# Transposing q and k on VectorE instead of TensorE in a windowed-attention and MLP kernel

## The chip, the cores and the metric

The kernel runs on one core of one Trainium2 chip. The metric is the time of one execution on the device in microseconds (us). The kernel before takes 755.5 us, the median of three runs (754.73 to 755.7).

The engines have the names of the profile: PE is TensorE (PEld its weight loads), DVE is VectorE, ACT is ScalarE, POOL is GpSimd, and SP is the engine whose queue issues nearly all DMAs.

## The reference

q, k and v have the shape (4 batches, 8 heads, 768 positions, 64), all float32. Attention is causal over a window of 128 positions, with the first 4 positions (the "sinks") always visible. The result goes through an MLP with 512 inputs and 2048 hidden units.

```
scores = scale * np.matmul(q, k.transpose(0, 1, 3, 2))
keep = is_sink | ((rel >= 0) & (rel < int(window)))
scores = np.where(keep, scores, -1000000000.0)
a = np.exp(scores - np.max(scores, axis=-1, keepdims=True))
a = a / (np.sum(a, axis=-1, keepdims=True) + 1e-09)
attn_out = np.matmul(a, v)                       # (B, H, S, D)
x = attn_out.transpose(0, 2, 1, 3).reshape(B * S, H * D)
h = x @ w_in
out = (h * (1.0 / (1.0 + np.exp(-h)))) @ w_out
```

## The kernel before

**Tiling.** The 4 x 768 rows of x are cut into eight *chunks* of 384 rows (CT = 384; a chunk is one half of one batch). Attention of a chunk is done in four *pairs* of heads, so there are 32 pairs, p = 0 to 31. The MLP of a chunk runs over 16 blocks of 128 hidden units (fc). For each block, `mlp1` (L834 to L846) makes 12 matmuls of 384 columns into an `h` tile, `act` (L848) lets ACT and DVE apply the activation, and `mlp2` (L860) adds 9 matmuls of 512 columns into three output banks. Each float32 product is split into a high and a low part in a narrower float32 format (fp32r), hence three matmuls where one would be expected.

**Two kinds of pair.** Pairs 0 to 7 (the first two chunks) go through functions whose names begin with `f_`; the change does not touch these functions. Pairs 8 to 31, the last six chunks, go through `load`, `q_prep`, `k_prep`, `v_prep`, `scores`, `softmax`, `ptrans`, `strans` and `av`. While the MLP of chunk c runs, the attention of chunk c + 2 runs between its matmuls.

**q and k.** `load` (L344) brings q and k of the two heads of a pair into SBUF as they lie in memory: a position on each of the 128 partitions, three blocks of positions for q (tile `qn`) and three or four for k (tile `kn`, four where the chunk is the second half of its batch and needs 128 keys of the first), and for each position the 64 numbers of one head beside the 64 of the other. The scores need the head dimension on the partitions. So `q_prep` (L381) has PE transpose each 128 x 128 block into the PSUM tile `qt` (L385), by a matmul against the identity, and `k_prep` (L402) does the same into `kt` (L408). ACT then copies the high parts from PSUM (L394, L395 for q; L422, L423 for k), and DVE subtracts them to get the low parts (L396, L397; L424, L425). For q, two more copies (L399, L400) fill the other half of `qd`. `scores` (L461, L465) are matmuls on these tiles.

**Buffers.** `qn` and `kn` have one buffer each, so a load of the next pair can start only when the transposes of this pair have read them. `qt`, `kt`, the score tiles, the transposed probabilities (`pt`, `sk`) and the attention outputs (`o`) share one PSUM tag, `at`, with three buffers that go round in the order in which the tiles are asked for.

**Order.** Each step is put on a list with a time (`at`), in units of one hidden block of the MLP (sixteen units to a chunk, four to a pair). The list is sorted by time and the steps are recorded in that order; a scheduling layer then fixes each engine's sequence of instructions, and at run time an engine never changes this sequence. The times are those in the table `OPT`: `a` has the offsets of the steps of a pair from that pair's own time T (`q`, `k`, `s` for the scores, `sm` for the softmax, `st` for `strans`, `av0` and `av1` for the two heads' outputs); `tk` the time at which the sinks are fetched; `wc` and `wcd` the start and the step of 32 range checks of the weights (`wchk`), each with a DMA of 512 KB and work on DVE and ACT.

Of the kernel before, what the change touches and what calls it, by code (L numbers as in the profile page):

```python
# [8 lines left out]
F32 = mybir.dt.float32  # L9
# [16 lines left out]

OPT = dict(
    S=7.834, s0=0.903, f_l=2.468, f_p=-1.643, f_v=3.079, f_sm=0.693, f_pt=0.795, f_av=0.052,
    tk=14.143, s1=1.65, F1=1.021, D0=2.076, w=[0.458, 8.623, 11.237, 18.219], wd=[0.839, 0.58,
    1.293, 0.683], wc=15.613, wcd=2.766, warm=7, wg=4, ord=1, edge=8, dua=15, adp=0, glp=0,  # L30
    ptv=9, fill=[0, 4, 0, 0, 1, 1, 0, 2], na=[2, 16], lod=[6, 30], a=dict(load=-2.705, q=0.041,
    k=-0.274, v=1.959, s=1.338, sd=0.33, sm=1.66, smd=0.624, pt0=3.456, st=3.466, pt1=3.482,
    av0=4.25, av1=4.394), m0=dict(act=0.606, m2=2.061), m=dict(act=0.378, m2=1.546), fin=0.692,
)


# [134 lines left out]
def attn_moe_kernel(  # L171
# [11 lines left out]
    nc = tc.nc  # L183
    B, H, S, D = q.shape
# [5 lines left out]
    P = 128  # L190
    HP = H // 2
    CT = 384
    NTB = CT // P
# [10 lines left out]
    ident = const.tile([P, P], F32, name="ident")  # L204
    make_identity(nc, ident)

    warm = OPT["warm"]
# [23 lines left out]
    with ExitStack() as fast:  # L231
        wpool = fast.enter_context(tc.tile_pool(name="wpool", bufs=1))
        p1 = fast.enter_context(tc.tile_pool(name="p1", bufs=1))
# [6 lines left out]
        m0 = p1.tile([P, P], F32, name="m0")  # L240
        m1 = p1.tile([P, WIN], F32, name="m1")
        m2 = p1.tile([P, WIN], F32, name="m2")
# [89 lines left out]
        st = [dict() for _ in range(NPER)]  # L332
# [6 lines left out]
        def geo(p):  # L339
            c, hp = divmod(p, HP)  # L340
            b, half = turns[c]
            return c, b, half, hp

        def load(p):  # L344
            c, b, half, hp = geo(p)
            s = st[p]
            r0 = half * CT
            s["qn"] = p1.tile([P, NTB, 2, D], F32, tag="qn", name=f"qn{p}")
            s["kn"] = p1.tile([P, NTB + 1, 2, D], F32, tag="kn", name=f"kn{p}")
            j0 = 0 if half else 1  # L350
            rk = r0 - P if half else r0
            for j in range(2):
                h = 2 * hp + j
                nc.sync.dma_start(
                    s["qn"][:, :, j, :], q[b, h, r0 : r0 + CT].rearrange("(t p) d -> p t d", p=P)
                )
                nc.sync.dma_start(
                    s["kn"][:, j0:, j, :], k[b, h, rk : r0 + CT].rearrange("(t p) d -> p t d", p=P)
                )

        def load_v(p):
            c, b, half, hp = geo(p)
# [18 lines left out]
        def q_prep(p):  # L381
            s = st[p]
            qt = ps_a.tile([P, 512], F32, tag="at", name=f"qt{p}")
            for t in range(NTB):
                nc.tensor.transpose(  # L385
                    qt[:, t * P : (t + 1) * P], s["qn"][:, t].rearrange("p h d -> p (h d)"), ident
                )
            qd = p1.tile([P, 2, CT], F32R, tag="qd", name=f"qd{p}")
            if "low" not in zero:
                zero["low"] = p1.tile([P, 2, CT], F32R, tag="ql", name="qlz")  # L390
                nc.gpsimd.memset(zero["low"].bitcast(F32), 0.0)
            ql = zero["low"]
            s["qd"] = qd
            nc.scalar.copy(qd[0:64, 0], qt[0:64, :CT])  # L394
            nc.scalar.copy(qd[64:128, 1], qt[64:128, :CT])  # L395
            nc.vector.tensor_tensor(ql[0:64, 0], qt[0:64, :CT], qd[0:64, 0], ALU.subtract)  # L396
            nc.vector.tensor_tensor(ql[64:128, 1], qt[64:128, :CT], qd[64:128, 1], ALU.subtract)  # L397
            eng = nc.gpsimd if p < OPT["dua"] else nc.vector
            eng.tensor_copy(qd[64:128, 0], qd[0:64, 0])  # L399
            eng.tensor_copy(qd[0:64, 1], qd[64:128, 1])  # L400

        def k_prep(p):  # L402
            c, b, half, hp = geo(p)
            s = st[p]
            j0 = 0 if half else 1
            kt = ps_a.tile([P, NTB + 1, P], F32, tag="at", name=f"kt{p}")
            for j in range(j0, NTB + 1):
                nc.tensor.transpose(  # L408
                    kt[:, j], s["kn"][:, j].rearrange("p h d -> p (h d)"), ident
                )  # L410
            ks = p1.tile([P, 2, (NTB + 1) * SEG], F32R, tag="ks", name=f"ks{p}")
            s["ks"] = ks
            ksv = ks.rearrange("p h (j c) -> p h j c", c=SEG)
            for j, src in ((0, ksA), (1, ksB)):
                n = NTB - j0
                nc.gpsimd.tensor_copy(  # L416
                    ksv[:, j, j0:NTB, P:],
                    src[:, hp, b, :].unsqueeze(1).to_broadcast([P, n, NS]),
                )
            A = ksv[:, 0, j0:, :P]  # L420
            Bk = ksv[:, 1, j0:, :P]
            nc.scalar.copy(A[0:64], kt[0:64, j0:])  # L422
            nc.scalar.copy(Bk[64:128], kt[64:128, j0:])  # L423
            nc.vector.tensor_tensor(A[64:128], kt[0:64, j0:], A[0:64], ALU.subtract)  # L424
            nc.vector.tensor_tensor(Bk[0:64], kt[64:128, j0:], Bk[64:128], ALU.subtract)  # L425
# [494 lines left out]
        for p in range(NPER):  # L920
            T = O["S"] + 4.0 * (p - HP)
            c, b, half, hp = geo(p)
# [26 lines left out]
            tl = T - 4.0 + max(A["k"] + 0.05, 4.0 + A["load"])  # L949
            tv = T - 4.0 + max(A["v"] + 0.05, 4.0 + A["load"])  # L950
            at(tl, lambda p=p: load(p))
            at(tv, lambda p=p: load_v(p))
            if hp == 0 and (c == 2 or b != turns[c - 1][0]):
                at(max(tv, O["tk"]) + 0.02, lambda b=b: load_vs(b))
            at(T + A["q"], lambda p=p: q_prep(p))
            at(T + A["k"], lambda p=p: k_prep(p))
            at(T + A["v"], lambda p=p: v_prep(p))
            for j in range(2):
# [12 lines left out]
        D0 = O["D0"]  # L971
# [51 lines left out]
```

## Time and profile before

| | before |
|---|---|
| median of three runs | 755.5 us (754.73 to 755.7) |
| profiled execution | 756.05 us |
| its span, first to last instruction | 754.3 us |
| granted TensorE clock, mean | 0.996 |
| busy: PE, PEld | 736.4 us (98%), 651.0 us (86%) |
| busy: DVE, ACT, POOL | 545.0 us (72%), 522.6 us (69%), 256.8 us (34%) |
| DMA | 98837 packets, 61.87 MB |

The span has three stages. Up to 139 us the eight early pairs are computed, the weights are read and split, and the MLP of the first chunk begins. From 139 us, where the first of the later pairs starts, to 682 us, where the seventh chunk is finished, the MLP and the later pairs run side by side. The last 72 us have the MLP of the last chunk alone.

One caution on PE rows: a matmul's duration in the profile runs from its start to its modelled end, and the next one starts before that end. What a matmul costs a busy PE is the distance from its start to the next start, not its duration.

### The profile page before, as it was taken

How to read it: one execution, taken by the hardware profiler on the slowest of the kernel's cores; microseconds unless marked ns; L12 is line 12 of the kernel's file. 1: busy time of each engine (PE TensorE's matmuls, PEld its weight loads, DVE VectorE, ACT ScalarE, POOL GpSimd, SP SyncE). 2: the span in 40 equal slices, each digit the busy share in tenths (PEclk: the TensorE clock that was granted, in tenths of full speed). 3: DMA queues.
4: the chain of work that ended last, by engine and by line, in shares of the span. 5: the costliest groups of instructions: out<-in, count | busy, mean ns of one | idle time of the engine just before them, and what ended most of it. 6: DMA issues, size and time to landing. Idle time of an engine off the chain costs nothing.

```text
span 754.3 us, 12661 instructions
## 1 busy us (share of the span) xinstructions
PE 736.4 (98%) x4068; PEld 651.0 (86%) x4068; DVE 545.0 (72%) x1435; ACT 522.6 (69%) x1195; POOL 256.8 (34%) x549
## 2 busy tenths in 40 slices
PE   7998999999999999999999999999999999999996
PEld 5676778789999999998999988999899999999885
DVE  5889788979767886678876797777876787752222
ACT  4879888588776776777866787767776777642222
POOL 3310000345454564534434453443433434330000
PEclk9999999999999999999999999999999999999999
DMA  7556454544111521025211450115311211001001
GB/s 177 167 153 182 129 152 146 159 132 149 27 41 40 168 78 36 20 69 159 70 40 40 123 150 16 34 32 153 112 35 39 84 39 40 1 1 43 0 1 44
DMA packets 98837, 61.87 MB, mean 82 GB/s; under 512 B 87504, under 2 KB 87504, under 8 KB 98768
## 3 DMA queue, kind: packets, MB, share of 16 engines
q1 hardware_dynamic: 98480, 61.03, 28.8%
q8 instruction: 33, 0.54, 0.3%
q14 instruction: 36, 0.29, 0.1%
q10 hardware_dynamic: 288, 0.00, 0.0%
HBM read 54.72 MB, written 6.29 MB: 81 GB/s over the span
## 4 chain that ended last, share of the span: by engine, by line
PE 81%; DVE 8%; DMA 4%; ACT 3%; issue 2%; SPq 1%; POOL 0%; DVEq 0%
PE h L843 30%; PE out L870 11%; PE out L871 11%; PE out L869 10%; PE o L574 3%; PE o L780 3%; DMA wraw<-in_moe_w_in_dram 2%; PE s L461 2%; PE s L465 2%; PE pt L516 2%; DMA wchk<-in_moe_w_out_dram 2%; PE s L715 1%; PE kt L408 1%; PE sk L547 1%; PE o L590 1%
## 5 line engine op out<-in xcount | busy, mean ns | idle before, releaser
L843 PE MATMUL h<-xh,winh 128*128 128x384 f32 x512 | 176.4, 345 | 0.0
L843 PE MATMUL h<-xl,winh 128*128 128x384 f32 x512 | 173.7, 339 | 0.0
L843 PE MATMUL h<-xh,winl 128*128 128x384 f32 x512 | 173.6, 339 | 0.0
L869 PE MATMUL out<-wouth,gh 128*128 128x512 f32 x384 | 152.9, 401 | 2.4 <-ACT gh L855 2.3
L870 PE MATMUL out<-wouth,gl 128*128 128x512 f32 x384 | 153.4, 400 | 0.6 <-DVE gl L857 0.6
L871 PE MATMUL out<-woutl,gh 128*128 128x512 f32 x384 | 153.0, 398 | 0.0
L854 DVE TENSOR_TENSOR sg<-h,sg 128x384 f32<-128x384 f32 x128 | 70.8, 554 | 82.4 <-ACT sg L853 81.4
L853 ACT ACTIVATE sg<-h 128x384 f32<-128x384 f32 x128 | 62.9, 492 | 81.4 <-PE h L843 79.4
L857 DVE TENSOR_TENSOR gl<-sg,gh 128x384 fp32r<-128x384 f32 x128 | 79.0, 617 | 31.2 <-ACT gh L855 29.5
L843 PEld LDWEIGHTS h<-xh,winh 128*128 128x128 f32 x512 | 96.5, 189 | 4.4 <-issue 0.6
L843 PEld LDWEIGHTS h<-xl,winh 128*128 128x128 f32 x512 | 96.3, 188 | 3.2
L843 PEld LDWEIGHTS h<-xh,winl 128*128 128x128 f32 x512 | 96.0, 188 | 1.1 <-issue 0.9
L855 ACT CAST gh<-sg 128x384 fp32r<-128x384 f32 x128 | 65.3, 510 | 39.1 <-DVE sg L854 37.7
L871 PEld LDWEIGHTS out<-woutl,gh 128*128 128x128 f32 x384 | 72.6, 189 | 17.2 <-issue 0.5
L869 PEld LDWEIGHTS out<-wouth,gh 128*128 128x128 f32 x384 | 72.0, 188 | 14.8 <-ACT gh L855 3.0
L870 PEld LDWEIGHTS out<-wouth,gl 128*128 128x128 f32 x384 | 72.7, 189 | 14.0 <-DVE gl L857 1.8
L532 POOL TENSOR_SCALAR_AFFINE_SELECT pq<-pq 128x384 fp32r<-128x384 f32 (+1 forms) x96 | 53.9, 570 | 63.0 <-ACT pq L525 63.0
L482 ACT ACTIVATE pm<-pm,mx 128x264 f32<-128x264 f32 (+1 forms) x144 | 71.3, 496 | 4.9 <-DVE mx L469 3.0
L502 POOL TENSOR_SCALAR pm<-pm,r 128x128 f32<-128x128 f32 x144 | 56.4, 409 | 34.4 <-DVE r L487 21.4
L469 DVE CUSTOM_DVE_ANT_0 pm<-s,m 128x264 f32<-128x264 f32 (+1 forms) x144 | 54.5, 408 | 13.2 <-PE s L465 12.7
L437 POOL TENSOR_TENSOR vs<-vn,vs 128x256 fp32r<-128x256 f32 (+1 forms) x48 | 35.4, 746 | 84.0 <-ACT vs L435 75.7
L416 POOL CAST ks<-ksA 128x24 fp32r<-128x24 f32 (+1 forms) x24 | 9.1, 378 | 160.6 <-PE s L465 98.7
(167 smaller groups left out, 1394.9 us busy)
## 6 DMA issues: line engine op xcount, KB each, us to landing
wraw<-in_moe_w_in_dram SPq DMA_DIRECT2D x16, 512.0 KB
wraw<-in_moe_w_out_dram SPq DMA_DIRECT2D x16, 512.0 KB
wchk<-in_moe_w_in_dram SPq DMA_DIRECT2D x16, 512.0 KB
wchk<-in_moe_w_out_dram SPq DMA_DIRECT2D x16, 512.0 KB
qn<-in_q_dram SPq DMA_DIRECT2D x64, 96.0 KB
kn<-in_k_dram SPq DMA_DIRECT2D x32, 128.0 KB
vn<-in_v_dram SPq DMA_DIRECT2D x32, 128.0 KB
out_dram<-ost SPq DMA_DIRECT2D x7, 512.0 KB
```

What stands on the lines that cost most here:

```text
L469: nc.vector.tensor_tensor_reduce(out=pm[:, t, off:], in0=sp[:, :w], in1=(m0, m1, m2)[min(blk, 2)], scale=-0.125, scalar=3.0e38, op0=ALU.ad ...
L482: nc.scalar.activation(x, x, AF.Exp, bias=mx[:, p, j * NTB + t : j * NTB + t + 1], scale=-1.0, accum_out=r[:, t : t + 1],)
L502: nc.gpsimd.tensor_scalar(x, x, r[:, t : t + 1], 1.0, ALU.mult, ALU.mult)
L532: nc.gpsimd.affine_select(out=before, in_=own, pattern=[[0, n], [-1, P]], compare_op=ALU.is_gt, fill=0.0, base=0, channel_multiplier=1,)
L843: nc.tensor.matmul(hps[:, :CT], w[g][:, cc, fs], s[x], start=n == 0, stop=n == 3 * NCC - 1)
L853: nc.scalar.activation(sg, hps[:, :CT], AF.Sigmoid)
L854: nc.vector.tensor_tensor(sg, hps[:, :CT], sg, ALU.mult)
L855: nc.scalar.copy(gh, sg)
L857: eng.tensor_tensor(gl, sg, gh, ALU.subtract)
L869: nc.tensor.matmul(o, gh[:, ts_], wout_h[g][:, f], start=fc == 0, stop=False)
L870: nc.tensor.matmul(o, gl[:, ts_], wout_h[g][:, f], start=False, stop=False)
L871: nc.tensor.matmul(o, gh[:, ts_], wout_l[g][:, f], start=False, stop=fc == NFC - 1)
```

## The change

`load` now cuts each head's 64 numbers into two halves of 32, and positions into blocks of 32. A DMA takes one half of one head: position within its block goes to 32 partitions, block number and the 32 numbers go along the row. Four DMAs each for q and k (two before) put the four groups of 32 head dimensions under one another. A run that lies together in memory is now 32 numbers long (128 bytes) where it was 64 (256 bytes). VectorE's transpose works on 32 x 32 blocks, each in its place; on this layout it gives what PE's transposes gave, head dimension on the partition and position along the row, in the same PSUM tiles `qt` and `kt`. So `q_prep` has one DVE instruction instead of three PE transposes, `k_prep` one instead of three or four. The rest of both functions is as it was. The table of times has new values: among them q's preparation is placed 0.61 units earlier and k's 0.2 later than before (below); `tk` goes from 14.143 to 16.284 and `wc` from 15.613 to 18.17, and `av0`, `av1` and `fin` by less than 0.5.

```diff
-    ptv=9, fill=[0, 4, 0, 0, 1, 1, 0, 2], na=[2, 16], lod=[6, 30], a=dict(load=-2.705, q=0.041,
-    k=-0.274, v=1.959, s=1.338, sd=0.33, sm=1.66, smd=0.624, pt0=3.456, st=3.466, pt1=3.482,
+    ptv=9, fill=[0, 4, 0, 0, 1, 1, 0, 2], na=[2, 16], lod=[6, 30], a=dict(load=-2.925, q=-0.567,
+    k=-0.079, v=1.964, s=1.3, sd=0.613, sm=1.795, smd=0.519, pt0=3.456, st=3.84, pt1=3.482,
...
-            s["qn"] = p1.tile([P, NTB, 2, D], F32, tag="qn", name=f"qn{p}")
-            s["kn"] = p1.tile([P, NTB + 1, 2, D], F32, tag="kn", name=f"kn{p}")
-            j0 = 0 if half else 1
+            s["qn"] = p1.tile([P, CT // 32, 32], F32, tag="qn", name=f"qn{p}")
+            s["kn"] = p1.tile([P, CT // 32 + 4, 32], F32, tag="kn", name=f"kn{p}")
+            j0 = 0 if half else 4
             rk = r0 - P if half else r0
             for j in range(2):
                 h = 2 * hp + j
-                nc.sync.dma_start(
-                    s["qn"][:, :, j, :], q[b, h, r0 : r0 + CT].rearrange("(t p) d -> p t d", p=P)
-                )
-                nc.sync.dma_start(
-                    s["kn"][:, j0:, j, :], k[b, h, rk : r0 + CT].rearrange("(t p) d -> p t d", p=P)
-                )
+                for e in range(2):
+                    to = slice(64 * j + 32 * e, 64 * j + 32 * e + 32)
+                    of = slice(32 * e, 32 * e + 32)
+                    nc.sync.dma_start(
+                        s["qn"][to],
+                        q[b, h, r0 : r0 + CT, of].rearrange("(i t) d -> t i d", t=32),
+                    )
+                    nc.sync.dma_start(
+                        s["kn"][to, j0:],
+                        k[b, h, rk : r0 + CT, of].rearrange("(i t) d -> t i d", t=32),
+                    )
...
-            for t in range(NTB):
-                nc.tensor.transpose(
-                    qt[:, t * P : (t + 1) * P], s["qn"][:, t].rearrange("p h d -> p (h d)"), ident
-                )
+            nc.vector.transpose(qt[:, :CT], s["qn"].rearrange("p i d -> p (i d)"))
...
-            for j in range(j0, NTB + 1):
-                nc.tensor.transpose(
-                    kt[:, j], s["kn"][:, j].rearrange("p h d -> p (h d)"), ident
-                )
+            nc.vector.transpose(
+                kt[:, j0:].rearrange("p t c -> p (t c)"),
+                s["kn"][:, 4 * j0 :].rearrange("p i d -> p (i d)"),
+            )
```

Three places show how the instructions stand, all around the preparation of pair 20, the first pair of the sixth chunk. In the kernel after, lines behind the edits have numbers that are 4 higher (L843 is L847, L854 is L858). The number behind a name only tells buffers apart.

PE, before: the transposes of k and q stand between the last matmuls of an `mlp2` and the first of an `mlp1`.

```order
L869 MATMUL out_2_4009<-wouth_145,gh_12_4728 128x512
L870 MATMUL out_2_4009<-wouth_145,gl_12_4729 128x512
L871 MATMUL out_2_4009<-woutl_146,gh_12_4728 128x512
L408 MATMUL kt_4804<-ident,kn_4634 128x128 x4
L385 MATMUL qt_4816<-ident,qn_4633 128x128 x3
L843 MATMUL h_14_4827<-xh_2994,winh_143 128x384
L843 MATMUL h_14_4827<-xl_2995,winh_143 128x384
```

PE, after, the same place between the two MLP steps:

```order
L873 MATMUL out_2_4004<-wouth_145,gh_12_4724 128x512
L874 MATMUL out_2_4004<-wouth_145,gl_12_4725 128x512
L875 MATMUL out_2_4004<-woutl_146,gh_12_4724 128x512
L551 MATMUL sk_4799<-ident,sx_4674 16x128 x2
L847 MATMUL h_14_4818<-xh_2999,winh_143 128x384
L847 MATMUL h_14_4818<-xl_3000,winh_143 128x384
```

The seven transposes are gone. The two transposes of the sink probabilities of pair 19 (`sk`), which stood an MLP step earlier, have moved here.

DVE, before: k's subtractions, q's, and the two copies of `qd` follow one another, behind the probabilities of pair 19 (`pq`) and ahead of its output (`x`).

```order
L857 TENSOR_TENSOR gl_13_4763<-sg_13_4761,gh_13_4762 128x384
L527 TENSOR_TENSOR pq_1_4788<-pt_1_4784,pq_1_4788 128x3x128
L424 TENSOR_TENSOR ks_4809<-kt_4804,ks_4809 64x4x128
L425 TENSOR_TENSOR ks_4809<-kt_4804,ks_4809 64x4x128
L396 TENSOR_TENSOR qlz<-qt_4816,qd_4820 64x384
L397 TENSOR_TENSOR qlz<-qt_4816,qd_4820 64x384
L399 COPY qd_4820<-qd_4820 64x384
L400 COPY qd_4820<-qd_4820 64x384
L599 TENSOR_TENSOR x_19_4840<-o_0_4841,x_19_4840 64x512
L854 TENSOR_TENSOR sg_14_4865<-h_14_4827,sg_14_4865 128x384
```

DVE, after: first q's transpose and subtractions, then further down k's.

```order
L391 STREAM_TRANSPOSE qt_4752<-qn_4607 128x384
L490 TENSOR_SCALAR r_1_4712<-r_1_4712 128x3
L503 TENSOR_TENSOR pm_1_4676<-pm_1_4676 128x2x128
L491 RECIPROCAL r_1_4712<-r_1_4712 128x3
L403 COPY qd_4754<-qd_4754 64x384
L858 TENSOR_TENSOR sg_12_4723<-h_12_4699,sg_12_4723 128x384
L400 TENSOR_TENSOR qlz<-qt_4752,qd_4754 64x384
L401 TENSOR_TENSOR qlz<-qt_4752,qd_4754 64x384
L861 TENSOR_TENSOR gl_12_4725<-sg_12_4723,gh_12_4724 128x384
L404 COPY qd_4754<-qd_4754 64x384
```

```order
L531 TENSOR_TENSOR pq_1_4783<-pt_1_4779,pq_1_4783 128x3x128
L861 TENSOR_TENSOR gl_13_4774<-sg_13_4772,gh_13_4773 128x384
L411 STREAM_TRANSPOSE kt_4804<-kn_4608 128x512
L559 TENSOR_TENSOR pst<-sk_4799,pst 16x256
L428 TENSOR_TENSOR ks_4806<-kt_4804,ks_4806 64x4x128
L429 TENSOR_TENSOR ks_4806<-kt_4804,ks_4806 64x4x128
L858 TENSOR_TENSOR sg_14_4842<-h_14_4818,sg_14_4842 128x384
```

q's part stands more than one hidden block earlier than before (ahead of the activation of block 12, where it stood behind that of block 13), amid the softmax of pair 19 (`r`, `pm`); the two transposes are new instructions, one in each part, and in each of them an activation of the MLP (`sg`) stands close behind.

SP, before: each pair has four loads of q and k and two of v.

```order
L357 DMA kn_4634<-in_k_dram 128x4x64
L354 DMA qn_4633<-in_q_dram 128x3x64 x2
L357 DMA kn_4634<-in_k_dram 128x4x64
L368 DMA vn_4700<-in_v_dram 128x4x64 x2
L357 DMA kn_4895<-in_k_dram 128x4x64
```

SP, after:

```order
L359 DMA qn_4607<-in_q_dram 32x12x32 x4
L363 DMA kn_4608<-in_k_dram 32x16x32 x4
L375 DMA vn_4696<-in_v_dram 128x4x64 x2
L359 DMA qn_4872<-in_q_dram 32x12x32 x4
L363 DMA kn_4873<-in_k_dram 32x16x32 x4
```

The loads of a pair have kept their place between the loads of v; there are eight of them, and all of q's stand ahead of k's.

More of the change, by code (lines that the diff above doesn't have):

```diff
@@ L28 @@
     S=7.834, s0=0.903, f_l=2.468, f_p=-1.643, f_v=3.079, f_sm=0.693, f_pt=0.795, f_av=0.052,
-    tk=14.143, s1=1.65, F1=1.021, D0=2.076, w=[0.458, 8.623, 11.237, 18.219], wd=[0.839, 0.58,
-    1.293, 0.683], wc=15.613, wcd=2.766, warm=7, wg=4, ord=1, edge=8, dua=15, adp=0, glp=0,
-    ptv=9, fill=[0, 4, 0, 0, 1, 1, 0, 2], na=[2, 16], lod=[6, 30], a=dict(load=-2.705, q=0.041,
-    k=-0.274, v=1.959, s=1.338, sd=0.33, sm=1.66, smd=0.624, pt0=3.456, st=3.466, pt1=3.482,
-    av0=4.25, av1=4.394), m0=dict(act=0.606, m2=2.061), m=dict(act=0.378, m2=1.546), fin=0.692,
+    tk=16.284, s1=1.65, F1=1.024, D0=2.076, w=[0.458, 8.623, 11.237, 18.219], wd=[0.839, 0.58,
+    1.293, 0.683], wc=18.17, wcd=2.694, warm=7, wg=4, ord=1, edge=8, dua=15, adp=0, glp=0,
+    ptv=9, fill=[0, 4, 0, 0, 1, 1, 0, 2], na=[2, 16], lod=[6, 30], a=dict(load=-2.925, q=-0.567,
+    k=-0.079, v=1.964, s=1.3, sd=0.613, sm=1.795, smd=0.519, pt0=3.456, st=3.84, pt1=3.482,
+    av0=4.289, av1=4.88), m0=dict(act=0.606, m2=2.061), m=dict(act=0.396, m2=1.546), fin=0.772,
 )
```

## The prediction

> **What bounds the kernel now.** I first read the busy times, and then asked for them over the stretch from 160 to 682 us, from the end of the first chunk to the end of the seventh, in which all changed pairs but the first lie. The columns are the busy us of PE, PEld, DVE, ACT and POOL, the granted clock, the DMA share and GB/s.
>
> ```profile
> PE 736.4 (98%) x4068; PEld 651.0 (86%) x4068; DVE 545.0 (72%) x1435; ACT 522.6 (69%) x1195; POOL 256.8 (34%) x549
> 160.00:682.00 522.00, 520.11 (x2993) 475.42 (x2992) 394.91 (x1025) 379.71 (x860) 229.05 (x501) 1.00 0.25 69
> PE 81%; DVE 8%; DMA 4%; ACT 3%; issue 2%; SPq 1%; POOL 0%; DVEq 0%
> ```
>
> PE is busy for 520.11 of 522 us at full clock, and the chain that ended last runs over PE for 81% of the span. DVE is busy for 394.91 us (76%) and has 127 us to spare. As a busy PE may still hide late starts, I looked at who holds PE up after 140 us; these are the longest of its waits there (us in total, times, longest).
>
> ```profile
> PEld o L574 <- POOL pq L536: 1.1, 1, 1.1
> PE o L574 <- DVE ks L425: 0.9, 1, 0.9
> PEld kt L408 <- DVE pq L527: 0.9, 2, 0.7
> ```
>
> No wait that the profile names is over 1.1 us. In this stretch the time is the sum of PE's slots: work taken from PE shortens it, as long as the other engines keep up.
>
> **PE: what goes.** The instructions are these, and the timeline of one pair shows what they hold up (start, duration).
>
> ```profile
> L408 PE MATMUL kt<-ident,kn 128*128 128x128 f32 x88 | 13.5, 272 | 0.3 <-DVE pq L527 0.3
> L385 PE MATMUL qt<-ident,qn 128*128 128x128 f32 x72 | 11.9, 275 | 0.0
> 404.22 0.39 PE L871 MATMUL out<-woutl,gh 128*128 128x512 f32 x1
> 404.45 0.60 PE L408 MATMUL kt<-ident,kn 128*128 128x128 f32 x4
> 404.88 0.49 PE L385 MATMUL qt<-ident,qn 128*128 128x128 f32 x3
> 405.13 0.42 PE L843 MATMUL h<-xh,winh 128*128 128x384 f32 x1
> 405.39 0.33 PE L843 MATMUL h<-xl,winh 128*128 128x384 f32 x1
> ...
> 410.60 0.40 PE L871 MATMUL out<-woutl,gh 128*128 128x512 f32 x1
> 410.84 0.34 PE L843 MATMUL h<-xh,winh 128*128 128x384 f32 x1
> 411.02 0.33 PE L843 MATMUL h<-xl,winh 128*128 128x384 f32 x1
> ```
>
> 88 and 72 make 160 transposes. Without transposes, `mlp1` follows `mlp2` with starts 0.24 and 0.18 us apart (410.60, 410.84, 411.02). With them, the second `mlp1` matmul starts at 405.39, which is 0.94 us after the first transpose; 0.18 of that is the first `mlp1` matmul's own slot. The seven transposes and the switch back cost 0.76 us, 0.109 us each. For 160 that is **17.4 us**. The mean durations of 272 and 275 ns would give 43.8 us, but they overlap.
>
> A place where the Trainium skill has another price: "TensorE: Matmul & The Clock Gate", Part 4 (PE-mode transpose), gives about 275 ns for a 128 x 128 transpose inside a kernel, which the durations here match. Charged as PE time it would take out 160 x 0.275 = 44 us by that page; the starts above say 17.4. I go by the starts, and it comes back as a rival.
>
> **DVE: what is added.** 24 transposes of 384 columns for q, and for k 16 of 512 and 8 of 384 (the eight pairs in first halves of a batch), all from SBUF to PSUM. The trace has no DVE instruction of this kind, and none that writes PSUM. The nearest are copies and subtractions of the same widths that read PSUM.
>
> ```profile
> L766 DVE COPY pTz<-pb 128x384 f32<-128x384 f32 x9 | 4.9, 543 | 0.3 <-PE pb L762 0.3
> L884 DVE COPY ost<-out 128x512 f32<-128x512 f32 x7 | 4.8, 692 | 3.0 <-PE out L871 3.0
> L397 DVE TENSOR_TENSOR qlz<-qt,qd 64x384 fp32r<-64x384 f32 x24 | 13.5, 561 | 0.3
> L425 DVE TENSOR_TENSOR ks<-kt,ks 64x512 fp32r<-64x512 f32 x16 | 11.1, 693 | 0.2
> ```
>
> 128 more columns cost 149 ns, one column per 1.16 ns, and both kinds agree within 18 ns, so I take the copies' price: 32 x 0.543 + 16 x 0.692 = **28.4 us**. From below, with a copy's fixed part alone (543 - 384 x 1.16 = 98 ns), it would be 5 us; from above, four passes over the data instead of one (98 + 4 x 445 = 1.88 us, and 2.47 us) make 100 us. As every one-pass row of this width lies at 0.54 to 0.69 us, I stay near them.
>
> At 28.4 us DVE is busy for 423 us of a stretch shortened to 505: 84%, with 81 us to spare instead of 127. So its work does not become the bound by its sum; it can by its order, since DVE takes its instructions in sequence. Behind each transpose stand an activation of the MLP (`sg`), on which ACT's `gh` and then `mlp2` depend, and the subtractions for which the scores wait. How PE looks when scores come late shows at one place in the trace.
>
> ```profile
> 435.11 0.28 PE L465 MATMUL s<-ks,qlz 128*128 128x264 f32 x1
> 435.23 0.28 PE L461 MATMUL s<-ks,qd 128*128 128x264 f32 x1
> ...
> 437.57 0.39 PE L871 MATMUL out<-woutl,gh 128*128 128x512 f32 x1
> 438.02 0.39 PE L461 MATMUL s<-ks,qd 128*128 128x264 f32 x1
> 438.24 0.28 PE L465 MATMUL s<-ks,qlz 128*128 128x264 f32 x1
> 438.37 0.39 PE L461 MATMUL s<-ks,qd 128*128 128x264 f32 x1
> ```
>
> Scores usually start 0.12 us apart; here the first starts 0.21 us late (0.45 after an `mlp2` matmul, not 0.24), and two follow after 0.22 in place of 0.12: some 0.4 to 0.5 us lost. If every one of the 24 pairs got one more such place, 12 us would go; if none, nothing. With DVE's spare share falling from 24% to 16%, and PE held up so little now, I charge a quarter: **3 us**.
>
> **The step that moves.** PE no longer needs `kn` and `qn`; the scores now wait for a chain that begins on DVE (transpose, two copies on ACT, two subtractions) instead of on PE. For k the links are 0.69 + 2 x 0.58 + 2 x 0.69 = 3.2 us by these rows and those below, where PE's four transposes took 0.6 for the first link.
>
> ```profile
> L422 ACT CAST ks<-kt 64x512 fp32r<-64x512 f32 x16 | 9.3, 580 | 19.0 <-PE kt L408 19.0
> 425.92 0.60 PE L408 MATMUL kt<-ident,kn 128*128 128x128 f32 x4
> ```
>
> The table plans k at -0.079 and the first scores at 1.3; a unit is 5.4 us (522 us for 96 units), so 7.5 us are planned for 3.2 us of links. What covers it is two steps of MLP on PE; a lateness over 4 us would come through to the scores. Cost: nothing, up to the 12 us already bounded. The PSUM buffers go round as before: `qt` and `kt` take buffers whose last readers stand ahead of them on DVE itself, so no new wait is expected there. The new times also reorder the last `f_` pairs before 139 us; PE is not full there, and I give this no term but 2 us either way in the range.
>
> **The loads.** A pair's loads are four DMAs now and eight after, with runs of 128 bytes. SP's issues of one pair (all four, then used by the transposes at 425.92), and queue 1 in the 8 us around them (packets, MB, share of 16 engines; v's loads are not yet among them):
>
> ```profile
> 405.08 0.37 SPq L357 DMA_DIRECT2D kn<-in_k_dram  x1
> 405.56 0.97 SPq L354 DMA_DIRECT2D qn<-in_q_dram  x2
> 406.58 0.48 SPq L357 DMA_DIRECT2D kn<-in_k_dram  x1
> q1 hardware_dynamic: 1856, 0.46, 25.6%
> ```
>
> They are issued 19 us before use. 1856 packets took 25.6% of 16 engines x 8 us, 17.7 ns each. After, eight issues take 3.9 us, and 3584 packets of half the size at most 3584 x 17.7 / 16 = 4.0 us, together 8 us at worst; the table gives the load 2.36 units (-2.925 to -0.567), 12.7 us. Hidden by a pair's worth of MLP: no cost. The cover ends where a packet takes more than about three times as long.
>
> Here the Trainium skill has a rule against the change: "DMA: Bandwidth & Descriptors", Specifications, says that below 512 bytes a DMA no longer runs at line rate, since it reads, modifies and writes. The 256-byte packets here already lie below that and do 14.5 GB/s per engine; no run shows 128 bytes. By the rule the halved runs could cost more than half of a packet's time, or more than all of it.
>
> **Sum.** Span 754.3 - 17.4 + 3 = 739.9 us. Around the span the profiled execution has 756.05 - 754.3 = 1.75 us, which gives 741.65; the median of the runs, 755.5, lies 0.55 us under the profiled time, which gives **741.1 us**, forecast 741.
>
> **Rivals.**
>
> *DVE holds PE up more.* The transposes cost twice the rows (57 us), DVE is busy for 452 of 505 us, 90%, and every pair loses the full 0.5 us: 755.5 - 17.4 + 12 = 750 us. For it: nearly every wait in the MLP's activation passes through DVE. Against: 16% spare at the price I take.
>
> *The transposes make DVE the bound, and the kernel slower.* At four passes, 100 us, DVE is busy for 495 us. If its sequence lets it be busy for no more than 90% (it has waits on ACT in every block), the stretch takes 550 us instead of 522: 755.5 + 28 = 783 us. It turns slower than before from 0.9 x 522 - 395 = 75 us, 2.6 times the rows' price. For it: no row shows what DVE takes to turn 32-bit blocks into PSUM. Against: the even slope of all its one-pass rows.
>
> *The loads come late.* If a packet of 128 bytes took five times 17.7 ns, a pair's loads would need 3584 x 88 / 16 = 20 us beside the issues, more than the 12.7 planned. DVE would stand at the head of its sequence waiting for q, some 7 us a pair, of which the 3 to 4 us of slack hide half: 24 x 3.5 = 84 us less the 14 gained, 826 us. For it: nothing here shows such packets. Against: 256-byte packets at 17.7 ns, with no sign of a step. The rule of the Trainium skill quoted above ("DMA: Bandwidth & Descriptors", Specifications) would come to this if it were that strong.
>
> *PE gains the full durations.* 755.5 - 43.8 = 712 us, if a transpose held PE for its whole duration. For it: the rows' means. Against: the starts, 0.109 us apart. The Trainium skill ("TensorE: Matmul & The Clock Gate", Part 4) reads this way.
>
> *Nothing gained.* The removed slots come back one for one, because some other engine's sequence sets the pace of a pair: 755 us. Against: PE's named waits are under 1.2 us each. That the change does other work than it says I exclude: it computes the same two PSUM tiles.
>
> **Chances.** Forecast 0.70 (its own range 735 to 746: no wait and 3 us of luck in the order, up to 8 us of waits), DVE holding PE up 0.13, DVE the bound 0.07, late loads 0.03, full durations 0.02, nothing gained 0.05. The range for 8 in 10 reaches from 734 to the first rival's 751. Faster by over 0.2% (about what a measurement here tells from no change, 1.5 us): 0.70 + 0.13 + 0.02 = 0.85; within it: 0.05; slower: 0.10.
>
> **What would show it.** After: no PE rows L385 and L408; 48 DVE transposes of 0.54 to 0.69 us, DVE near 84% between the chunks' ends; these ends 84.1 us apart in place of 87; PE still busy to 99%, and its waits on DVE at 3 us more in sum. The q and k packets doubled at 17.7 ns or less, with no DVE wait on a DMA at the transposes. Transposes over 1.4 us, or DVE waiting on `qn` or `kn`, would make the prediction wrong.

## The result, and the profile after

The kernel after takes 734.95 us (median; 733.97 to 735.01), the kernel before 755.6 us (754.73 to 756.9). The ratio is 0.9721, with an interval of 0.9701 to 0.9741: 20.6 us less, where 14 were forecast. The profiled execution took 733.97 us, its span 732.3 (before 756.05 and 754.3). One more execution of the kernel after, of 1415 us, is left out; its cause is not known, and no run of any other kernel here shows one like it.

The page after: busy times, the chain that ended last, and then the window from 160 to 660 us, roughly the first to the seventh end of a chunk (columns as in the prediction).

```profile
PE 717.0 (98%) x3908; PEld 632.4 (86%) x3908; DVE 556.5 (76%) x1483; ACT 526.5 (72%) x1197; POOL 255.0 (35%) x549
...
PE 91%; DVE 2%; DMA 2%; ACT 1%; SPq 1%; POOL 1%; issue 1%; DVEq 0%; POOLq 0%
...
160.00:660.00 500.00, 499.36 (x2825) 455.47 (x2824) 405.08 (x1070) 379.13 (x855) 225.09 (x498) 1.00 0.30 72
```

PE has 160 matmuls fewer (3908 for 4068) and is busy for 499.36 of 500 us; DVE has 48 instructions more and is busy for 81% of the window. The chain runs over PE for 91% of the span instead of 81%: PE bounds the kernel more than before. Where the 22 us of span went is read from the copy that ends each chunk, the view of its tile before and after (shortest/median/longest in ns, first and last start):

```profile
L884 DVE COPY ost<-out x7: 691/691/693, 160.0 to 682.2; 128x512 f32<-128x512 f32 x7
```

```profile
L888 DVE COPY ost<-out x7: 670/691/692, 157.3 to 660.4; 128x512 f32<-128x512 f32 x7
```

2.7 us came ahead of the first end. The six chunks between take 503.1 us instead of 522.2, 83.9 us apart for 87.0: 19.1 us. Behind the last end 72 us remain as before.

The new instructions in the groups after (busy us, mean ns of one):

```profile
L391 DVE STREAM_TRANSPOSE qt<-qn 128x384 f32<-128x384 f32 x24 | 13.8, 574 | 0.0
L411 DVE STREAM_TRANSPOSE kt<-kn 128x512 f32<-128x512 f32 x16 | 11.4, 715 | 0.0
L411 DVE STREAM_TRANSPOSE kt<-kn 128x384 f32<-128x384 f32 x8 | 4.6, 580 | 0.0
```

Together 29.8 us of DVE. Of the waits that stand under PE after 140 us only one is left (before there were five; its weight loads, PEld, still have some, none over 0.9 us):

```profile
PE o L578 <- POOL pq L540: 0.5, 1, 0.5
```

To see what the change did to PE's slots, I added up in each trace, from 100 us on, the distances from one matmul's start to the next one's start, by the tile of the first. This gives a gap in front of a late matmul to the matmul ahead of it. Differences to the kernel before, in us; "span" is that of the profiled execution.

| counted to | after | old order (E1) | PE, new order (E2) | q early (E5) | o late (E12) | q only (E3) | k only (E4) | one group (E9) |
|---|---|---|---|---|---|---|---|---|
| `kt`, `qt` | -15.9 | -15.9 | +1.0 | -15.9 | -15.9 | -8.0 | -8.1 | -15.9 |
| `sk` | -2.0 | 0 | +9.8 | +6.6 | 0 | 0 | -2.0 | +7.1 |
| `pt` | +0.2 | 0 | +0.1 | +1.2 | 0 | +0.2 | +1.7 | +2.7 |
| `o` | -1.1 | +13.0 | -2.0 | +3.3 | -1.8 | -1.6 | +0.8 | -1.8 |
| `s` | -1.8 | +0.8 | -1.8 | -1.3 | +13.8 | +0.9 | +0.1 | -2.2 |
| `out` | -0.7 | +12.5 | +0.5 | +2.0 | +3.8 | -0.3 | +0.9 | -1.3 |
| `h` | -0.3 | -2.5 | +0.9 | -1.3 | -2.7 | +1.0 | +1.2 | -1.8 |
| span | -22.0 | +7.6 | +8.5 | -5.5 | -3.0 | -8.6 | -5.8 | -13.7 |

One thing has to be known to read the rows. Within a group of transposes the starts lie 0.109 us apart in both traces, but the last one is followed after 0.03 us already, and the matmul behind the group then holds its slot 0.08 us longer (0.26 us for `h` instead of 0.18). So 0.08 us of a group are counted to another tile; a group of n transposes still costs n x 0.109. A pair has two groups before (`pt0`, `sk`, `pt1`, and `kt`, `qt`) and two after (`pt0`, `pt1`, and `sk` alone). The -2.0 of `sk` (24 x 0.08) is therefore no wait that went, but part of what the removed transposes cost; where nothing stands in their place (E1, E12), the same 2 us are missing under `h`. In the kernel after, the removed transposes give 15.9 + 2.0 = 17.9 us, and the other gaps together 3.7 us more. What the new table of times has to do with that is what the experiments are about.

### The profile page after: what moved, and what is told of

The parts are those of the page before. It is cut to its first block, busy times and chain, and to the rows that moved or that the text cites. A ratio compares the mean times of both kernels' runs of the same rounds, so it can differ in the third digit from the quotient of the medians.

```text
span 732.3 us, 12472 instructions
## 1 busy us (share of the span) xinstructions
PE 717.0 (98%) x3908; PEld 632.4 (86%) x3908; DVE 556.5 (76%) x1483; ACT 526.5 (72%) x1197; POOL 255.0 (35%) x549
## 4 chain that ended last, share of the span: by engine, by line
PE 91%; DVE 2%; DMA 2%; ACT 1%; SPq 1%; POOL 1%; issue 1%; DVEq 0%; POOLq 0%
PE h L847 36%; PE out L874 12%; PE out L875 12%; PE out L873 12%; PE o L578 4%; PE o L784 3%; PE s L465 2%; PE s L469 2%; PE pt L520 2%; DMA wraw<-in_moe_w_in_dram 2%; PE s L719 1%; PE o L594 1%; PE o L587 1%; PE sk L551 1%; SPq L645 1%
## 5 line engine op out<-in xcount | busy, mean ns | idle before, releaser
L847 PE MATMUL h<-xh,winh 128*128 128x384 f32 x512 | 177.1, 346 | 0.0
L847 PE MATMUL h<-xl,winh 128*128 128x384 f32 x512 | 173.9, 340 | 0.0
L847 PE MATMUL h<-xh,winl 128*128 128x384 f32 x512 | 173.3, 338 | 0.0
L858 DVE TENSOR_TENSOR sg<-h,sg 128x384 f32<-128x384 f32 x128 | 71.0, 554 | 61.6 <-ACT sg L857 59.9
L847 PEld LDWEIGHTS h<-xh,winh 128*128 128x128 f32 x512 | 96.6, 189 | 3.9 <-issue 0.9
L847 PEld LDWEIGHTS h<-xl,winh 128*128 128x128 f32 x512 | 96.2, 188 | 2.0
L847 PEld LDWEIGHTS h<-xh,winl 128*128 128x128 f32 x512 | 96.1, 188 | 0.6 <-issue 0.5
L861 DVE TENSOR_TENSOR gl<-sg,gh 128x384 fp32r<-128x384 f32 x128 | 74.3, 580 | 18.3 <-ACT gh L859 17.6
L873 PEld LDWEIGHTS out<-wouth,gh 128*128 128x128 f32 x384 | 72.0, 188 | 14.4 <-ACT gh L859 2.7
L506 POOL TENSOR_SCALAR pm<-pm,r 128x128 f32<-128x128 f32 x144 | 58.5, 422 | 45.3 <-DVE r L491 26.9
L536 POOL TENSOR_SCALAR_AFFINE_SELECT pq<-pq 128x384 fp32r<-128x384 f32 (+1 forms) x96 | 52.9, 561 | 53.8 <-ACT pq L529 53.8
L540 POOL TENSOR_SCALAR_AFFINE_SELECT pq<-pq 128x384 fp32r<-128x384 f32 (+1 forms) x96 | 49.7, 529 | 6.3 <-DVE pq L531 4.1
```

The lines of the kernel that those rows point to most:

```text
L506: nc.gpsimd.tensor_scalar(x, x, r[:, t : t + 1], 1.0, ALU.mult, ALU.mult)
L536: nc.gpsimd.affine_select(out=before, in_=own, pattern=[[0, n], [-1, P]], compare_op=ALU.is_gt, fill=0.0, base=0, channel_multiplier=1,)
L847: nc.tensor.matmul(hps[:, :CT], w[g][:, cc, fs], s[x], start=n == 0, stop=n == 3 * NCC - 1)
L858: nc.vector.tensor_tensor(sg, hps[:, :CT], sg, ALU.mult)
L861: eng.tensor_tensor(gl, sg, gh, ALU.subtract)
L873: nc.tensor.matmul(o, gh[:, ts_], wout_h[g][:, f], start=fc == 0, stop=False)
```

## The experiments

The scheduling layer puts some neighbouring instructions in another order for every edit, so a difference of a microsecond or two between two kernels is not read as the edit's own. The kernel before, run beside them, had medians of 754.9 to 755.7 us. Each ratio is to it.

**E1 and E2: the two parts of the change apart.** E1 is the kernel after with the table of times of the kernel before; E2 is the kernel before with the table of the kernel after.

```diff
 E1, in after (E2, in before: the same lines the other way round)
-    ptv=9, ..., a=dict(load=-2.925, q=-0.567,
-    k=-0.079, v=1.964, s=1.3, sd=0.613, sm=1.795, smd=0.519, pt0=3.456, st=3.84, pt1=3.482,
-    av0=4.289, av1=4.88), ...
+    ptv=9, ..., a=dict(load=-2.705, q=0.041,
+    k=-0.274, v=1.959, s=1.338, sd=0.33, sm=1.66, smd=0.624, pt0=3.456, st=3.466, pt1=3.482,
+    av0=4.25, av1=4.394), ...
 (and tk, F1, wc, wcd, m, fin)
```

> The change with the table of times of the kernel before: q and k are loaded in 32 x 32 blocks and transposed by DVE, but all steps keep their old times. Theory A (slots): the 160 transposes give back 0.109 us each, 17.4 us, whatever the order; what was gained beyond that (21.0 us in all, so 3.6) comes from the new times. This run: 755.6 - 17.4 = 738 us, up to 741 with a few waits. Theory B (order): most of the gain is the new order; with the old one DVE comes too late and the run stays above 746 us. Theory C (joint): old times and DVE transposes do not fit, PE waits for DVE at the scores, 741 to 746 us.

> The kernel before with the table of times of the kernel after: PE transposes, old loads, new times. Theory A: the new times alone are worth 3.6 us: 752 us. Theory B: they are worth most of the gain: below 745 us. Theory C: they pay only together with the DVE transposes: 755.6 us or more here.

Measured: E1 765.4 us, ratio 1.0131 (1.0114 to 1.0148); E2 764.89 us, 1.0125 (1.0109 to 1.0142). Each part alone makes the kernel slower by about 10 us, and both together faster by 21. E1 gets the same 17.9 us from the transposes (15.9, and 2.0 of the 2.5 under `h`) and loses 25 behind `o` and `out` (table). Its page, and its longest waits after 140 us:

```profile
PE 724.1 (95%) x3908; PEld 633.0 (83%) x3908; DVE 564.9 (74%) x1483; ACT 523.7 (69%) x1195; POOL 254.0 (33%) x549
...
PE o L578 <- DVE ks L429: 16.1, 23, 1.4
PEld o L578 <- issue: 10.7, 10, 1.7
```

The second `o` of a pair waits 23 times for `ks`. But `o` reads `pq` and `vs`; it does not read `ks`. So this is no wait for data. The tiles `qt`, `kt`, `s`, `pt`, `sk` and `o` share one PSUM pool of three buffers (`ps_a`, tag "at"), and a tile takes the buffer of the tile asked for three before it. What it waits for is that tile's last reader, and `ks` is the last reader of `kt`. The order in which PE fills them, from the timelines:

| kernel | order of one pair | `o` and `s` take the buffers of |
|---|---|---|
| before, E1 | `pt0`, `sk`, `pt1`, `kt`, `qt`, `o0`, `o1`, `s`... | `o0` of `pt1`; `o1` of `kt`; first `s` of `qt`, next of `o0`, `o1` |
| after | `qt`, `pt0`, `pt1`, `sk`, `kt`, `o0`, `o1`, `s`... | `o0` of `pt1`; `o1` of `sk`; first `s` of `kt`, next of `o0`, `o1` |

In the old order `o1` needs `kt`'s buffer. On PE the transposes of `kt` stood at 404.45 us (prediction), and `ks` was read from it at 406.99, ahead of the second `o` at 408.02. In E1 the same pair shows on the timeline of DVE and PE:

```profile
408.05 0.55 DVE L531 TENSOR_TENSOR pq<-pt,pq 128x384 fp32r<-128x384 f32 x1
408.52 0.71 DVE L411 STREAM_TRANSPOSE kt<-kn 128x512 f32<-128x512 f32 x1
...
411.17 0.69 DVE L429 TENSOR_TENSOR ks<-kt,ks 64x512 fp32r<-64x512 f32 x1
...
411.17 0.40 PE L874 MATMUL out<-wouth,gl 128*128 128x512 f32 x1
411.92 0.74 PE L578 MATMUL o<-pq,vs 128*128 128x256 f32 x4 [0.35 <-DVE ks L429]
412.49 0.28 PE L587 MATMUL o<-pq,vs 128*128 128x256 f32 x1
```

The transpose now stands in DVE's sequence, behind `pq`, and cannot start as early as PE's did. `ks` is done at 411.86, and `o` starts at 411.92, 0.75 us behind an `mlp2` matmul whose successor usually follows after 0.23. The bracket counts 0.35 as idle, since the matmul before it is still running for 0.40.

E2 has the new order with PE's transposes, and there `kt` stands three behind `pt0`, whose last reader is the subtraction `pq`:

```profile
PE kt L408 <- DVE pq L527: 7.1, 17, 0.7
...
PEld kt L408 <- DVE pq L527: 12.2, 18, 1.0
```

`kt` reads `kn` and the identity, not `pq`: a buffer again. On PE the transpose holds up everything behind it. With the transpose on DVE, `pq` and the transpose are in one sequence and PE does not see it. That fits why the new order is bad for the one and good for the other: it takes `o1` off `kt`'s buffer, and it puts `kt` behind `pq`, where DVE stands anyway.

**E5 and E12: single steps from the old order to the new.** E5 is E1 with q's preparation at its new time only, E12 is E1 with the second `o` at its new time only.

```diff
 E5, in E1
-    ... a=dict(load=-2.705, q=0.041,
+    ... a=dict(load=-2.705, q=-0.567,
 E12, in E1
-    av0=4.25, av1=4.394), ...
+    av0=4.25, av1=4.88), ...
```

> The e1 kernel (DVE transposes, old table) with one number changed: q's step is placed at -0.567 instead of 0.041, so that kt no longer shares its PSUM buffer with the second head's output o of the pair before. Theory D (buffer ring): e1's loss is that o takes the buffer of kt three tiles on, and waits for the last subtraction of k; with q moved ahead o takes a buffer that is long free, and the 16 us of PE waiting for that subtraction go: 765.4 - 16 to 20 = 745 to 749 us. Theory E (DVE is simply late with all its work in the old order): the change of one step's place does little, 760 us or more.

> The e1 kernel (DVE transposes, old table) with one other number changed: the second head's output, the step that waited there, is placed at 4.88 (the new table's value) instead of 4.394, which puts a whole mlp2 (2.1 us of PE work) between the first head's output and the second's. Nothing of q or k moves. Theory D (buffer ring): the wait for kt's last reader, at most 1.6 us a pair, is covered by this work; most of e1's loss beyond the kernel after goes, 740 to 748 us, unless the scores behind now wait for the later output in their turn. Theory E (DVE late with everything): 760 us or more.

Measured: E5 751.12 us, 0.9957 (0.9941 to 0.9974); E12 754.09 us, 0.9983 (0.9972 to 0.9995). Either step takes away the wait of E1 (14.3 and 11.3 us), and each puts another in its place, E5's first and then E12's:

```profile
PE pt L520 <- DVE qlz L401: 4.7, 8, 1.0
PE o L578 <- POOL pq L540: 2.1, 6, 0.7
PEld pt L520 <- DVE qlz L401: 6.8, 11, 1.3
```

```profile
PE s L465 <- DVE x L603: 8.3, 13, 1.4
PEld s L465 <- DVE x L603: 11.4, 14, 1.6
```

`pt` does not read `qlz`, nor `s` read `x`. In E5 the order is `qt`, `pt0`, `sk`, `pt1`, so the second `pt` gets `qt`'s buffer, which `qlz` reads last (the table counts this gap to `sk`, which stands ahead of it); in E12 `o` comes later, and the scores that take its buffers wait for its readers. In the kernel after both steps are taken and `sk` stands behind both `pt`: `sk` then takes `qt`'s buffer, later, and no such wait is left. Neither of the two steps brings the gain alone; which of the table's other values it needs was not tried, nor was a fourth buffer for the tag, which would be the direct test of the ring.

**E9: one group moved.** The kernel after with q 0.6 units earlier still and the step `st` at its old place.

```diff
-    ... q=-0.567,
+    ... q=-1.2,
-    ... st=3.84, ...
+    ... st=3.469, ...
```

> The kernel after with two numbers changed: q's step still earlier (-0.567 to -1.2) and the sinks' transposes (st 3.84 to 3.469) put between the two heads' transposes, so that PE has one group of transposes per pair instead of two. In the traces the matmul behind each group starts some 0.08 us late; 24 groups fewer are worth 24 x 0.08 = 2 us, if q's readers are done when the second head's pt takes qt's buffer. Theory D (buffer ring, with room): 733 us. If q's early transpose pushes DVE's softmax work back or the ring closes again, 737 us or more.

Measured 742.31 us, 0.9829 (0.9806 to 0.9851), 7.4 us worse than after. The 2 us hoped for do not exist: `h` has 1.8 us less, but the 0.08 us behind a group belong to its last transpose, which holds that much longer when another transpose follows. And the `sk` gap of E5 is back (+7.1 in the table), with the same row for it:

```profile
PE pt L520 <- DVE qlz L401: 3.9, 12, 0.7
```

**E3 and E4: q alone, k alone, in the new order.**

```diff
 E3: k loaded by rows and transposed on PE as before (E4: q instead)
-            nc.vector.transpose(kt[:, j0:]..., s["kn"][:, 4 * j0 :]...)
+            for j in range(j0, NTB + 1):
+                nc.tensor.transpose(kt[:, j], s["kn"][:, j]..., ident)
```

> The kernel after, with k loaded and transposed on PE as before (88 transposes back on PE, q's 72 on DVE). Theory A: 735 + 88 x 0.109 = 744.5 us. Theory B: within 2 us of the kernel after, 735 to 737. If a switch of PE between transposes and other matmuls, rather than the transposes' number, costs the time, half the switches remain and the run lies at 735 + 10.5 = 745 or more in both this and the k-only run.

> The kernel after, with q loaded and transposed on PE as before (72 transposes back on PE, k's 88 on DVE). Theory A: 735 + 72 x 0.109 = 742.8 us, 1.7 us below the q-only run. Theory B: 735 to 737 us. If one of the two (q or k) made the whole difference, one of these two runs would lie at 735 and the other near 752.

Measured: q alone 747.15 us, 0.9887 (0.987 to 0.9903); k alone 750.05 us, 0.9922 (0.9905 to 0.9939). The transposes' share does add up: 8.0 us for q's 72, and for k's 88 8.1 with the 2.0 under `sk`, 10.1 us; together 18.1 for 17.9. The rest does not: the other gaps come to +0.2 us with q alone and +4.7 with k alone, and to -3.7 with both. With k alone, PE's remaining `qt` meets waits of the same sort again (`sk` for the reader of `qt`):

```profile
PE sk L553 <- DVE qlz L403: 1.2, 2, 0.8
```

**E6 and E7: what DVE may cost.** Each DVE transpose is done twice (E6) or four times (E7) into the same tile, which is repeated work and nothing else.

```diff
-            nc.vector.transpose(qt[:, :CT], ...)
+            for _ in range(2):        # 4 in E7
+                nc.vector.transpose(qt[:, :CT], ...)
 (the same for kt)
```

> The kernel after with every DVE transpose made twice, into the same place: 48 more instructions, 29.8 us more DVE work by their durations. Theory D: DVE has idle time, and the chain from kt to the scores has some 4 us of slack in the new order, so two to three quarters of a us more do not reach PE: 735 to 739 us. Theory F (DVE is nearly the bound already): each added us of DVE work costs about a us, 755 to 765 us.

> The kernel after with every DVE transpose made four times: 89 us more DVE work, the price of the prediction's slower rival. DVE then has 423.6 + 86 = 510 us of work in a stretch of 522 us (the stretch from 139 to 661 us of the kernel after). If DVE can be busy for no more than 90%, as the rival said, the stretch becomes 566 us: 735 + 44 = 779 us. If it can run at nearly 100%, 735 to 745 us. A waiting chain alone (2 us more per pair at q and at k, slack 4 us) would give 740 to 750 us.

Measured: E6 742.69 us, 0.9838 (0.9822 to 0.9855); E7 761.85 us, 1.0091 (1.0071 to 1.0112). With 29.8 us more of DVE the kernel is 7.7 us longer, with 89.4 us more 26.9. The new waits in E7 after 140 us, and its busy times by window:

```profile
PEld s L467 <- DVE x L605: 10.9, 18, 1.1
PEld out L876 <- DVE gl L863: 7.9, 17, 0.8
...
PE s L467 <- DVE x L605: 6.7, 12, 0.9
...
160.00:690.00 530.00, 517.85 (x2851) 461.71 (x2850) 483.25 (x1212) 385.82 (x866) 225.58 (x505) 1.00 0.28 69
```

PE is still busy for 98% of the window, and DVE for 91%. So neither a full DVE nor a step was reached; the time rises along with lateness at single places, first the buffer of `o` again, then the MLP's `gl`. On a straight line between E6 and E7 the gain is gone at 70 us of added DVE work, 100 us in all, 3.3 times the real price.

**E8: shorter runs.** The same loads in pieces of 16 floats, 64 bytes, twice as many DMAs.

```diff
-                    nc.sync.dma_start(s["qn"][to], q[b, h, r0 : r0 + CT, of]...)
+                    for g in range(0, 32, 16):
+                        nc.sync.dma_start(s["qn"][to, :, g : g + 16], q[b, h, r0 : r0 + CT, 32 * e + g : 32 * e + g + 16]...)
 (the same for k)
```

> The kernel after with each load of q and k cut in two along the head dimension: runs of 64 bytes in place of 128, twice the packets and sixteen issues a pair. Theory: the loads are hidden by most of a pair's 20.6 us, and a packet costs less the shorter it is (17.8 ns at 256 bytes, 12.6 ns at 128 bytes in the traces, so about 10 ns): 7168 x 10 / 16 = 4.5 us and 8 us of issue: 735 us, no change. The rival of late loads: packets below some size cost far more, DVE waits at its transposes for a DMA, 745 us or more.

Measured 735.15 us, 0.9732 (0.9716 to 0.9749): no difference to the kernel after. Queue 1 of the kernel after, over 3 us in which only q's loads run, and then over the whole span; and of E8 over the whole span (packets, MB, share of 16 engines):

```profile
q1 hardware_dynamic: 1200, 0.15, 30.1%
...
q1 hardware_dynamic: 140976, 61.04, 32.8%
```

```profile
q1 hardware_dynamic: 225968, 61.05, 37.4%
```

30.1% of 16 x 3 us over 1200 packets is 12.0 ns for 128 bytes. From 100 us to the end the means are 17.8 ns for 256 bytes (before), 12.6 for 128 (after) and 10.0 for 64 (E8): half the bytes cost 0.7 to 0.8 of the time, with no step. DVE waits for no load at the transposes in either kernel.

**E10 and E11: more of the same.** E10 also loads and transposes q and k of pairs 4 to 7, the later four of the `f_` pairs, in this way: eight DVE transposes more, 24 on PE fewer. E11 is E10 and E9 together.

```diff
 f_load and f_prep, for p >= HP: block loads as in the last chunks, and
-            (three PE transposes of each of q and k)
+            nc.vector.transpose(dst[:, :CT], src[:, : CT // 32].rearrange("p i d -> p (i d)"))
```

> The kernel after with pairs 4 to 7 (the second chunk, through the f_ functions) loaded and transposed in the same way: 24 PE transposes fewer, 8 DVE transposes more, at 75 to 139 us, where PE is not full and DVE has 43 of 50 us of work. If PE's slots set the time there too: 24 x 0.1 = 2.4 us less, 732.5 us. If DVE or the loads set it: 735 us, or some us more.

> The two edits above together. If they act at different places they add: 735 less what each of them gained, 730.5 us if both do as hoped.

Measured: E10 747.07 us, 0.9884 (0.9869 to 0.9899); E11 755.71 us, 1.0001 (0.9992 to 1.001). E10 loses 12.1 us of the gain, E9 7.4, and E11 20.8, for 19.5 in sum: the losses add. In the window from 75 to 139 us, after and then E10:

```profile
75.00:139.00 64.00, 63.85 (x328) 51.06 (x327) 53.37 (x137) 56.49 (x125) 4.75 (x7) 1.00 0.52 145
```

```profile
75.00:139.00 64.00, 59.40 (x282) 46.06 (x282) 49.62 (x128) 51.08 (x109) 1.34 (x4) 0.96 0.54 138
```

PE was already full there and is no longer: it loses 4.5 us of busy time, and its granted clock falls from 1.00 to 0.96. E10's waits between 70 and 145 us name DVE and ACT in the MLP (`h` for `sg` 2.6 us, `out` for `gh` 1.9, each once). All of E10's loss lies in this first part: its first chunk ends at 173.2 us (157.3 after), and the six chunks behind it take 500.1 us, 3.0 less than after. Why DVE and ACT come late there was not traced further, and no times that suit this form were tried; so E10 shows that the same edit loses under the given times, not that it must.

## Why the prediction was right, and where not

**PE bounds, and work taken from it shortens the time: shown.** All kernels of the table with q and k on DVE have the same 15.9 us less in `kt` and `qt`, whatever their total. The chunk ends came 83.9 us apart for 84.1 forecast (a figure without the 3 us of waits), and the time was 735 us, inside the range, at the lower edge of its likeliest part (735 to 746), 6 us under the forecast.

**The transposes' term, 17.4 us, held:** 17.9 in the rows, 0.112 us each for 0.109; half a microsecond is less than two kernels differ by anyway. The timeline after, at the place where pair 20's transposes were:

```profile
393.58 0.39 PE L875 MATMUL out<-woutl,gh 128*128 128x512 f32 x1
393.81 0.38 PE L551 MATMUL sk<-ident,sx 128*16 128x128 f32 x2
393.95 0.42 PE L847 MATMUL h<-xh,winh 128*128 128x384 f32 x1
394.21 0.34 PE L847 MATMUL h<-xl,winh 128*128 128x384 f32 x1
394.39 0.34 PE L847 MATMUL h<-xh,winl 128*128 128x384 f32 x1
```

Two transposes take 0.14 us here, one 0.109 and the last 0.03, and the first `mlp1` matmul holds its slot for 0.26 us, not 0.18: the same as behind the seven before (405.13 to 405.39). What the prediction called the switch back is what the last transpose's own slot lacks, so its price, measured up to the second `mlp1` matmul, was the right one. The mean duration of a transpose, 272 ns, was not, so that rival is out. The Trainium skill's 275 ns ("TensorE: Matmul & The Clock Gate", Part 4) agrees with the duration and not with the time freed.

**The DVE term was right:** 29.8 us for 28.4, durations 0.57 to 0.72 for 0.54 to 0.69, DVE 81% for 84%. Turning blocks into PSUM costs about what a copy of that width costs. Over the span DVE's busy time grew by 11.5 us only (545.0 to 556.5), since other instructions of its became shorter, `gl` from 617 to 580 ns in the mean; why was not asked. The rival in which DVE is the bound was priced too high: four passes were to give 783 us and a loss from 2.6 times the price; E7 did more than that and gave 762, and the break-even lies near 3.3 times. The first rival's case, twice the price and 750 us, was E6: 743.

**The waits were wrong in sign.** The prediction charged 3 us more; the gaps outside the transposes fell by 3.7 us (table, the rows from `pt` to `h`). These 6.7 us, 0.5 of the transposes and 0.4 from before 100 us are the 7.6 us between its 14.4 and the 22.0 of the span. What it had wrong is the premise that "the PSUM buffers go round as before". What it drew from it for `qt` and `kt` held: `kt` takes the buffer of `pt0`, whose last reader `pq` stands ahead of it on DVE. But the ring does not go round as before: the new table changes which tile follows which, and in the old order the same transposes on DVE cost 25 us in waits (E1), at the second `o`. The gain hangs on both parts: 765 us without the new order, 765 without the transposes on DVE, 735 with both. The prediction took the table's part to be the planned times of q and k with 4 us of slack to the scores; the scores were not what came late. It never asked what else stood in `kt`'s buffer. So the right time is in part luck: no term of its sum depends on the order, and the same sum for E1 would have been 24 us too low.

**The loads were hidden: shown,** by E8 with runs of half that length and twice the DMAs. The packets of 128 bytes took 12.0 to 12.6 ns, below the 17.7 assumed. The Trainium skill's rule on descriptors under 512 bytes ("DMA: Bandwidth & Descriptors", Specifications) does not show as a step between 256 and 64 bytes, all of them below its limit, and no run here shows the limit itself; what the same page says under "Why small descriptors are slow (HBM only)", a fixed part of about 3 cycles per packet, would give (4 + 3)/(8 + 3) = 0.64 for half of 256 bytes, an estimate, and the runs gave 0.67 to 0.71 (12.0 and 12.6 for 17.8).

**The reorder of the first phase,** given 0 with 2 us either way, brought 2.7 us by the first chunk's end, of which 0.8 are transposes removed ahead of it; all are part of the sums above. The reason given, that PE is not full before 139 us, does not hold for the end of that phase: in the kernel before PE is busy for 63.75 of 64 us from 75 to 139.

**Which waits fell.** From 145 us on the trace before has eleven slots that are over 0.1 us longer than usual (0.18 us for `h`, 0.23 for `out`, 0.12 for `s` and `o`), 4.4 us in all; the trace after has three, 1.3 us. The longest is the 1.1 us in front of the second `o` of pair 21 (452.26 to 453.49 us), the prediction's row of `o` for `ks`: its input `pq` was ready at 452.88, the last reader of its buffer, `ks`, done at 453.33, so about half of it is the buffer's. The 0.4 us of `kt` for `pq` are a wait for a buffer too; no row after has either. Others are inputs that come late (`s` for `qlz` at 150 us, `out` for `gl` at 349). Each of them is a single place in one trace, so how much of the 3.7 us the order earned, and how much is the chance of neighbouring instructions, stays open.

## What to carry to other kernels

When a step moves to another engine, write down for every PSUM or SBUF ring it takes part in which tile takes whose buffer, and when that tile's last reader is done in the new engine's sequence; where a named releaser is no input of the waiting instruction, look whether it is the last reader of the tile that had the buffer before. Try such a move together with a new order: either part alone was 10 us slower here, and both together 21 us faster. Price work taken from a full engine by the distances of starts, up to the second instruction behind the group, and not by durations.

## What was not expected of the hardware

VectorE turned 32 x 32 blocks of 32-bit floats from SBUF into PSUM at 574 ns for 128 x 384 and 715 ns for 128 x 512, one column in 1.1 ns, about the speed of its copies (1.16). DMA packets of 64 bytes took 10.0 ns and of 256 bytes 17.8, so runs four times shorter cost 2.2 times the engine time per byte, and in E8 nothing at all in the kernel's time. The last transpose of a group is followed after 0.03 us instead of 0.109, and the matmul behind it holds its slot 0.08 us longer, behind the two of `sk` as behind the seven of q and k; so joining groups of transposes saves nothing.
